# A Fourier filter and a routed expert layer on one core: the turn and the inverse of the first two batches in separate PSUM banks, a shorter last chain of the list, and noise products in another order

## The chip, the cores and the metric

The kernel runs on one core of a Trainium2 chip. The metric is the device time of one execution in microseconds. The three runs of the kernel before took 2244.74, 2246.81 and 2250.58 us, so the median is 2246.81 us. A profile of one more execution is used throughout; its times are counted from the start of its span.

## What is computed

The reference filters eight batches of 2496 x 256 numbers in the Fourier domain, and then sends each of the 19968 rows to two of eight experts:

```python
X = np.fft.rfft(x, axis=1)
y = np.fft.irfft(X * (filt_r + 1j * filt_i), n=x.shape[1], axis=1)
x = y.reshape(B * S, D)
logits = x @ w_gate
noise_scale = np.log1p(np.exp(x @ w_noise))
noisy_logits = logits + noise_scale * noise
top2 = the two largest of noisy_logits in each row
weights = softmax over these two
out[row] += weight * (relu(x[row] @ w1[e]) @ w2[e])   # for both experts e of the row
```

## The kernel before, in words

**Work and stages.** The transform of 2496 points is cut into 39 x 64. A batch passes a first DFT matmul (`s1`, names q1 and u3 in the profile), a second one with the filter (`kg1`, q3), the way back through the 64 points (`kg2`, q4, into the tile G), and then `t3` (q5: the *turn*, four transposes of G, evicted by ScalarE as `tf`) and `i2` (q6: the *inverse* DFT, evicted by ScalarE as `yt`, and written to `y` in DRAM). `t3` is line 512 on TensorE, `i2` is line 534. `gate` then takes the logits of a batch (`lg`, line 493), adds the scaled noise, finds the two experts of each row and their weights, counts rows (`rs`), and needs three tiny matmul groups on the way: `rk` (lines 812 to 814, ranks and counts), `sl` (883 and 884, first slots of blocks) and `st` (908, the table of slots). Behind them, VectorE copies the table to `tabi` (line 916), which SyncE and GpSimd read. `route` builds the batch's list of rows with comparisons (`oc`) and matmuls (`ra`), transposes it (line 957), finishes it on VectorE (lines 962 to 966) and scatters it to the DRAM tensor `lst` from GpSimd (line 969). `expert` reads lists, gathers rows, and runs both matmuls of an expert on blocks of 512 rows (lines 123 to 125 by way of `_mm3`, and 1210 and 1211).

**What sets the order.** The first two batches are transformed ahead of the first expert. Their work is written out in `fft_stream` in a table of slots: for slot `t` the functions in `plan[t]` are called in turn, and `pin` keeps every engine's instructions in the order in which they are written. Batch 0 has its turns and inverses in slots 12 to 17, batch 1 in slots 26 to 31. The gate of batch 1 is called in slot 26, with `hold=False`: its instructions are not held to that order, and a scheduler, which simulates the program, places them among the others. In that same slot `gating_more` is called until `rk`, `sl` and `st` have been written out too. So their PSUM tiles are allocated in slot 26, ahead of those of slot 27.

**PSUM.** There are eight banks, in four pools: `hps` with 2, `yps` with 2, `xps` with 1 and `fps` with 3. For the first two batches `EARLY` and `MOVES` say in which pool a name has its bank; a name that stands in neither has `fps`. `lg`, `u2`, `rk`, `sl`, `st` and `ra` are such names. `MOVES[14]` holds from slot 14 on, `MOVES[26]` from slot 26 on:

```python
EARLY = {"q1": "hps", "q2": "hps", "q5": "yps", "q6": "yps", "u1": "xps", "u3": "hps"}
BANKS = {"hps": 2, "yps": 2, "xps": 1, "fps": 3}
self.banks.update(MOVES.get(t, {}))
```

A tile gets a bank of its pool when an earlier tile in that bank has been used for the last time; tiles of a pool are served in the order in which the program allocates them.

Of the kernel before, what the change touches and what calls it, by code (L numbers as in the profile page):

```python
# [10 lines left out]
F32 = mybir.dt.float32  # L11
# [5 lines left out]
ALU = mybir.AluOpType  # L17
# [36 lines left out]
LR = 128  # L54
NLR = 1536
VAIN = 1400
HR = 56
# [80 lines left out]
EARLY = {"q1": "hps", "q2": "hps", "q5": "yps", "q6": "yps", "u1": "xps", "u3": "hps"}  # L138
BANKS = {"hps": 2, "yps": 2, "xps": 1, "fps": 3}

MOVES = {0: {"q3": "yps"}, 12: {"q3": "fps"}, 14: {"q3": "yps", "q4": "yps", "q5": "hps", "q6": "hps"}, 26: {"q1": "xps", "q4": "fps", "q5": "yps", "q6": "yps"}}


class Moe:
# [412 lines left out]
    def fft_stream(self):  # L557
# [105 lines left out]
        for t in range(max(plan) + 1):  # L663
            self.banks.update(MOVES.get(t, {}))
            for g in plan.get(t, []):
# [78 lines left out]
    def gate(self, bt, lgp):  # L744

        nc, P, v = self.nc, self.P, self.nc.vector
        sh = [RP, NG, E]

        def t(nm, s=None, dt=F32):
            return P.tile(s or sh, dt, name=nm)  # L750

        lg = lgp[:RP, :352].rearrange("p (g e) -> p g e", e=16)
        noise = t("noise")
        nc.sync.dma_start(noise, self.io["noise"][bt])
        A, B = self.rank
        u, w, l, z = A[:, 17:], B[:, 16:], t("gl"), t("gz")
# [3 lines left out]
        nc.scalar.activation(l, w, AF.Ln)  # L760
        v.tensor_scalar_add(w, w, -1.0)
        v.tensor_single_scalar(z, w, 0.0, op=ALU.is_equal)
        v.tensor_add(l, l, z)
        v.tensor_add(w, w, z)
        v.reciprocal(w, w)
        v.tensor_mul(l, l, w)
        v.tensor_mul(l, l, u)
        v.tensor_mul(l, l, noise)
        nz = t("gz")
        v.tensor_add(nz, l, lg[:, :, 0:8])  # L770
        keyb = self.key[:RP].unsqueeze(1).to_broadcast(sh)
# [26 lines left out]
        src, o = A, B  # L798
        for k in 1, 2, 4, 8, 16:
            v.tensor_add(o[:, 16:38], src[:, 16:38], src[:, 16 - k:38 - k])  # L800
            src, o = o, src
        src, o = src[:, 16:38], A[:, 17:]
# [8 lines left out]
        q = self.ps("rk")  # L811
# [41 lines left out]
        ri, rf = t("ri", [HR, 1], I32), P.tile([HR, 1], F32, name="rf", bufs=2)  # L853
# [64 lines left out]
    def route(self, bt, hi, lo, row, rf):  # L918


        nc, P = self.nc, self.P

        def bc(a, n):
            return a.rearrange("p g i -> p (g i)").unsqueeze(1).to_broadcast([RP, n, 4])


        x, v = P.tile([128, LR], F32, name="rx"), nc.vector
        xs = x[:, :HR]
        lr, tv = self.half[:RP, :4 * LR].rearrange("p (l j) -> p l j", j=4), self.half[:RP, 4 * LR:]
        for g0 in range(0, NG, 4):  # L930
            q = self.ps("ra")[:, :HR]
            for g in range(g0, min(g0 + 4, NG), 2):
                t = P.tile([128, 1024], F16, name="oc", tag=("xh", "xl", "b")[g // 2 % 3], bufs=1)


                ol, vv = t[:RP, 0:4 * LR], t[:RP, 4 * LR:4 * LR + 4 * HR]
                if bt < 2:
                    ol, vv = (a.rearrange("p (l j) -> p l j", j=4) for a in (ol, vv))
                else:
                    ol, vv = (a.rearrange("p (j l) -> p l j", j=4) for a in (ol, vv))  # L940

                def w(a):
                    return a if bt < 2 else a.rearrange("p l j -> p j l")

                v.tensor_tensor(w(vv), w(lr[:, :HR]), w(bc(hi[:, g:g + 2], HR)), op=ALU.is_equal)
                v.tensor_mul(w(vv), w(vv), w(tv[:, 2 * g:2 * g + 4].unsqueeze(1).to_broadcast([RP, HR, 4])))
                v.tensor_tensor(w(ol), w(lr), w(bc(lo[:, g:g + 2], LR)), op=ALU.is_equal)
                for j in range(4):
                    n = RP if g + j // 2 < NG - 1 else QA
                    nc.tensor.matmul(q, ol[:n, :, j], vv[:n, :, j], start=(g == g0 and j == 0), stop=(j == 3 and g + 2 >= min(g0 + 4, NG)))  # L950
            if g0 == 0:
                v.tensor_copy(xs, q)
            else:
                v.tensor_add(xs, xs, q)
            yield
        q = self.ps("ra")[:HR, :LR]
        nc.tensor.transpose(q, xs, self.ident)
        x = x[:HR]


        o = P.tile([HR, LR], F32, name="ro", **(dict(tag="th", bufs=3) if bt < 2 else dict(tag="ut1", bufs=1)))
        v.tensor_single_scalar(o, q, 0.0, op=ALU.not_equal)
        v.scalar_tensor_tensor(o, lr[:HR, :, 0], rf, o, op0=ALU.add, op1=ALU.mult)
        v.tensor_sub(o, q, o)
        v.tensor_single_scalar(x, q, 0.0, op=ALU.is_gt)
        v.tensor_sub(o, o, x)
        self.made = bt
        yield
        s = nc.gpsimd.indirect_dma_start(
            out=self.lst, out_offset=bass.IndirectOffsetOnAxis(ap=row[:, 0:1], axis=0),  # L970
            in_=o, in_offset=None, compute_op=ALU.add)
        for r in self.reads:
            self.tc.declare_no_dep(s.ins, r.ins, reason="what is read was complete a batch ago")
        self.writes.append((bt, s))
        yield
# [66 lines left out]
    def take(self, ent):  # L1042

        xg, at, ra = ent[2]
        gate = self.P.tile([128, 4, 1], F32, name="gt", bufs=3)[:, :len(xg)]
        self.nc.gpsimd.tensor_copy(gate, self.picked(ent)[:, :, D:][:, :, bass.ds(ra, 1)])
        return gate
# [287 lines left out]
```

## Time and profile before

| | us |
|---|---|
| median of 3 runs | 2246.81 |
| profiled execution, its device time | 2249.04 |
| its span, first to last instruction | 2247.3 |
| TensorE busy | 2202.3 |
| VectorE busy | 1614.5 |
| ScalarE busy | 1227.9 |
| GpSimd busy | 945.7 |

Busy time is that in which an engine has an instruction running. PE stands for TensorE, DVE for VectorE, ACT for ScalarE, POOL for GpSimd and SP for SyncE. A row of a timeline gives the start in us, the time from the start of the first to the end of the last instruction of the row, the engine, the line of the kernel, the operation, the tile written and the tiles read, their sizes, and how many instructions the row holds; in brackets stands how long the engine had been idle before it, and what ended that. The granted clock is the share of TensorE's full clock that it was given.

### The profile page before, as it was taken

How to read it: one execution, taken by the hardware profiler on the slowest of the kernel's cores; microseconds unless marked ns; L12 is line 12 of the kernel's file. 1: busy time of each engine (PE TensorE's matmuls, PEld its weight loads, DVE VectorE, ACT ScalarE, POOL GpSimd, SP SyncE). 2: the span in 40 equal slices, each digit the busy share in tenths (PEclk: the TensorE clock that was granted, in tenths of full speed). 3: DMA queues.
4: the chain of work that ended last, by engine and by line, in shares of the span. 5: the costliest groups of instructions: out<-in, count | busy, mean ns of one | idle time of the engine just before them, and what ended most of it. 6: DMA issues, size and time to landing. Idle time of an engine off the chain costs nothing.

```text
span 2247.3 us, 39485 instructions
## 1 busy us (share of the span) xinstructions
PE 2202.3 (98%) x12687; PEld 1847.3 (82%) x12687; DVE 1614.5 (72%) x3482; ACT 1227.9 (55%) x2415; POOL 945.7 (42%) x824
## 2 busy tenths in 40 slices
PE   8999999999999999999999999999999999999998
PEld 6658888888888888888888888878888888888887
DVE  4777778779877968797668857796555556667776
ACT  6475655665565456545554445544444344557776
POOL 4014335334433543444434534444545454544442
PEclk9999999999999999999999999999999999999999
DMA  8768778987887677666665657556555557787774
GB/s 246 229 198 221 190 174 182 211 212 166 196 195 180 150 167 170 142 158 155 145 153 125 147 116 174 111 124 122 110 125 114 126 109 156 154 209 201 208 197 127
DMA packets 435434, 370.57 MB, mean 165 GB/s; under 512 B 185643, under 2 KB 345363, under 8 KB 435219
## 3 DMA queue, kind: packets, MB, share of 16 engines
q1 hardware_dynamic: 373907, 283.58, 46.7%
q0 software_dynamic: 61312, 84.40, 23.4%
q8 instruction: 101, 1.65, 0.3%
q14 instruction: 114, 0.93, 0.1%
HBM read 227.73 MB, written 105.25 MB: 148 GB/s over the span
## 4 chain that ended last, share of the span: by engine, by line
PE 89%; DVE 3%; DMA 3%; ACT 2%; issue 2%; SPq 0%; POOL 0%; another core or an unknown queue 0%; POOLq 0%; DVEq 0%; ACTq 0%
PE yps L1210 20%; PE hps L123 13%; PE hps L125 13%; PE hps L124 12%; PE yps L1211 10%; PE q L446 3%; PE yps L125 3%; PE yps L123 3%; PE yps L124 3%; PE q L512 1%; DMA stage<-w 1%; PE u L459 1%; PE q L536 1%; PE q L329 1%; PE q L534 1%
## 5 line engine op out<-in xcount | busy, mean ns | idle before, releaser
L1218 POOL DMA_INDIRECT out<-stage,ids x316 | 535.7, 1695 | 415.8 <-DVE stage L1217 224.4
L1210 PE MATMUL yps<-w,hh 128*128 128x512 f32 x1952 | 690.2, 398 | 4.0 <-DVE stage L1217 2.6
L1027 POOL DMA_INDIRECT stage<-y,ids x316 | 328.5, 1040 | 582.8 <-DMA xt<-stage 424.6
L124 PE MATMUL hps<-mxl,w1h 128*128 128x512 f32 (+2 forms) x1424 | 529.7, 374 | 1.5 <-DVE mxl L1091 1.5
L123 PE MATMUL hps<-mxh,w1h 128*128 128x512 f32 (+2 forms) x1424 | 518.9, 377 | 5.2 <-DVE hl L1182 3.7
L125 PE MATMUL hps<-mxh,w1l 128*128 128x512 f32 (+2 forms) x1424 | 523.9, 370 | 0.0
L1211 PE MATMUL yps<-w,hl 128*128 128x256 f32 x1952 | 521.7, 281 | 0.0
L1182 DVE SCALAR_TENSOR_TENSOR hl<-hps,hh 128x512 fp32r<-128x512 f32 (+2 forms) x712 | 433.5, 624 | 97.4 <-ACT hh L1181 88.1
L1181 ACT ACTIVATE hh<-hps 128x512 fp32r<-128x512 f32 (+2 forms) x712 | 381.5, 555 | 183.4 <-PE hps L125 163.6
L1210 PEld LDWEIGHTS yps<-w,hh 128*128 128x128 f32 x1952 | 356.7, 188 | 82.2 <-issue 5.3
L1211 PEld LDWEIGHTS yps<-w,hl 128*128 128x128 f32 x1952 | 367.1, 188 | 26.3 <-issue 0.6
L1215 ACT ACTIVATE stage<-yps,gt 128x256 f32<-128x256 f32 x316 | 142.3, 478 | 348.9 <-PE yps L1211 177.8
L125 PEld LDWEIGHTS hps<-mxh,w1l 128*128 128x128 f32 x1424 | 268.0, 188 | 48.1
L123 PEld LDWEIGHTS hps<-mxh,w1h 128*128 128x128 f32 x1424 | 263.4, 188 | 50.5 <-DVE hl L1182 9.1
L124 PEld LDWEIGHTS hps<-mxl,w1h 128*128 128x128 f32 x1424 | 268.1, 188 | 42.8 <-DVE mxl L1091 2.0
L1217 DVE SCALAR_TENSOR_TENSOR stage<-yps,gt,stage 128x256 f32<-128x256 f32 x244 | 112.1, 479 | 215.7 <-ACT stage L1215 185.3
L1137 ACT CAST w1h<-stage 128x512 fp32r<-128x512 f32 x192 | 119.2, 622 | 113.2 <-DMA stage<-w 52.9
L1138 DVE TENSOR_TENSOR w1l<-stage,w1h 128x512 fp32r<-128x512 f32 x192 | 130.8, 686 | 56.7 <-ACT w1h L1137 46.6
L123 PE MATMUL yps<-w,hh 128*128 128x256 f32 x576 | 163.4, 288 | 4.0 <-ACT hh L1181 3.0
L125 PE MATMUL yps<-w,hl 128*128 128x256 f32 x576 | 159.2, 285 | 1.1 <-DVE hl L1182 1.1
L124 PE MATMUL yps<-w,hh 128*128 128x256 f32 x576 | 160.1, 284 | 0.0
L1138 DVE TENSOR_TENSOR w<-stage,w 128x512 fp32r<-128x512 f32 x228 | 152.7, 685 | 6.7 <-ACT w L1137 5.3
(231 smaller groups left out, 3044.4 us busy)
## 6 DMA issues: line engine op xcount, KB each, us to landing
stage<-w SPq DMA_DIRECT2D x420, 256.0 KB
x<-x SPq DMA_DIRECT2D x88, 256.0 KB
wb<-w SPq DMA_DIRECT2D x18, 1024.0 KB
fx<-fd SPq DMA_DIRECT2D x140, 128.0 KB
fd<-c SPq DMA_DIRECT2D x73, 240.0 KB
out<-z SPq DMA_DIRECT2D x24, 702.0 KB
y<-yt SPq DMA_DIRECT2D x40, 248.6 KB
y<-yt SPq DMA_DIRECT2D x40, 234.0 KB
```

Of the source, the lines that this page charges most:

```text
L123: nc.tensor.matmul(o, lh, rh, start=start, stop=False)
L124: nc.tensor.matmul(o, lh, rl, start=False, stop=False)
L125: return nc.tensor.matmul(o, ll, rh, start=False, stop=stop)
L1027: self.pin(lambda: nc.gpsimd.indirect_dma_start(out=x.bitcast(I32), out_offset=None, in_=self.y[:BLK + ready * ROWS], in_offset=bass.Indir ...
L1137: nc.scalar.copy(h, sv)
L1138: nc.vector.tensor_sub(l, sv, f32v(h))
L1181: r = nc.scalar.activation(h, p, AF.Relu)
L1182: v = nc.vector.scalar_tensor_tensor(l, p, 0.0, f32v(h), op0=ALU.max, op1=ALU.subtract)
L1210: nc.tensor.matmul(bank, h, hl, start=(f == 0), stop=False)
L1211: self.mm = nc.tensor.matmul(p, l, hl[:, 0], start=False, stop=(f == 7))
L1215: nc.scalar.activation(o, p, AF.Copy, scale=gate[:, t])
L1218: a = nc.gpsimd.indirect_dma_start(out=self.io["out"][:BLK + ready * ROWS], out_offset=bass.IndirectOffsetOnAxis(ap=ids[:, t:t + 1], axis= ...
```

## The change

It has three parts. From slot 14 the turn (q5) has its bank in `xps` in place of `hps`, and from slot 26 in `fps` in place of `yps`; the inverse (q6) stays in `hps` and then `yps`. In `gate` the factor 1/(w - 1) is multiplied with `u` and with the noise before it meets the logarithm. In `route` the sum of position and row offset is formed ahead of the transpose, and behind the transpose three instructions stand in place of five.

```diff
-MOVES = {0: {"q3": "yps"}, 12: {"q3": "fps"}, 14: {"q3": "yps", "q4": "yps", "q5": "hps", "q6": "hps"}, 26: {"q1": "xps", "q4": "fps", "q5": "yps", "q6": "yps"}}
+MOVES = {0: {"q3": "yps"}, 12: {"q3": "fps"}, 14: {"q3": "yps", "q4": "yps", "q5": "xps", "q6": "hps"}, 26: {"q1": "xps", "q4": "fps", "q5": "fps", "q6": "yps"}}
...
         nc.scalar.activation(l, w, AF.Ln)
         v.tensor_scalar_add(w, w, -1.0)
         v.tensor_single_scalar(z, w, 0.0, op=ALU.is_equal)
-        v.tensor_add(l, l, z)
         v.tensor_add(w, w, z)
         v.reciprocal(w, w)
+        v.tensor_mul(w, w, u)
+        v.tensor_mul(w, w, noise)
+        v.tensor_add(l, l, z)
         v.tensor_mul(l, l, w)
-        v.tensor_mul(l, l, u)
-        v.tensor_mul(l, l, noise)
...
+        o = P.tile([HR, LR], F32, name="ro", **(dict(tag="th", bufs=3) if bt < 2 else dict(tag="ut1", bufs=1)))
+        v.tensor_scalar(o, lr[:HR, :, 0], rf, None, op0=ALU.add)
         q = self.ps("ra")[:HR, :LR]
         nc.tensor.transpose(q, xs, self.ident)
         x = x[:HR]
-        o = P.tile([HR, LR], F32, name="ro", **(dict(tag="th", bufs=3) if bt < 2 else dict(tag="ut1", bufs=1)))
-        v.tensor_single_scalar(o, q, 0.0, op=ALU.not_equal)
-        v.scalar_tensor_tensor(o, lr[:HR, :, 0], rf, o, op0=ALU.add, op1=ALU.mult)
+        v.scalar_tensor_tensor(x, q, 0.0, o, op0=ALU.not_equal, op1=ALU.mult)
+        v.scalar_tensor_tensor(o, q, 0.0, x, op0=ALU.is_gt, op1=ALU.add)
         v.tensor_sub(o, q, o)
-        v.tensor_single_scalar(x, q, 0.0, op=ALU.is_gt)
-        v.tensor_sub(o, o, x)
```

Beside what the diff shows, the change moves instructions on the engines. The first place is TensorE in slots 26 and 27, in the second batch's turns and inverses. Before, the turns and inverses go on behind the two matmuls of line 329 (q1 and u3, the first DFT of the third batch):

```order
L534 MATMUL q6_1320<-tf_1306,cm_84 117x512
L329 MATMUL q1_1326<-x_1101,cm_84 120x512
L329 MATMUL u3_1331<-x_1103,cm_84 120x512
L512 MATMUL q5_1420<-ident_70,G_974 120x128 x4
L534 MATMUL q6_1427<-tf_1318,cm_84 117x512
L512 MATMUL q5_1432<-ident_70,G_974 120x128 x4
L534 MATMUL q6_1439<-tf_1425,cm_84 117x512
```

The matmuls of `rk` of the same batch stand behind ten more rows, among the first expert's transposes (xps); `sl` and `st` stand later still, among that expert's matmuls:

```order
L1087 MATMUL xps_1759<-ident_70,stage_83 128x128 x4
L512 MATMUL q5_1484<-ident_70,G_1128 120x128 x4
L812 MATMUL rk_1336<-rs_1280,small_77 117x8
L813 MATMUL rk_1336<-rs_1280,small_77 128x8
L814 MATMUL rk_1336<-small_77,rs_1280 8x1
L534 MATMUL q6_1491<-tf_1467,cm_84 117x512
```

In the changed kernel, at the same place on TensorE as in the first of these two:

```order
L534 MATMUL q6_1319<-tf_1305,cm_84 117x512
L329 MATMUL q1_1325<-x_1100,cm_84 120x512
L329 MATMUL u3_1330<-x_1102,cm_84 120x512
L812 MATMUL rk_1335<-rs_1279,small_77 117x8
L813 MATMUL rk_1335<-rs_1279,small_77 128x8
L814 MATMUL rk_1335<-small_77,rs_1279 8x1
L883 MATMUL sl_1393<-new_1386,small_77 8x1
L884 MATMUL sl_1393<-new_1386,small_77 8x1
L908 MATMUL st_1414<-sval_1403,small_77 1x64
L512 MATMUL q5_1419<-ident_70,G_973 120x128 x4
L534 MATMUL q6_1426<-tf_1317,cm_84 117x512
L512 MATMUL q5_1431<-ident_70,G_973 120x128 x4
```

All three groups of the gate have moved ahead of the fourth turn of the batch.

The second place is VectorE in the gate of the second batch, from w - 1 to the sum with the logits (`rank38` and `rank39` hold w and u, `gl` the logarithm, `w1l` the low halves of the first expert's weights). Before:

```order
L761 TENSOR_SCALAR rank38_95<-rank38_95 117x176
L762 TENSOR_SCALAR gz_1242<-rank38_95 117x176
L763 TENSOR_TENSOR gl_1241<-gl_1241,gz_1242 117x176
L764 TENSOR_TENSOR rank38_95<-rank38_95,gz_1242 117x176
L765 RECIPROCAL rank38_95<-rank38_95 117x176
L1138 TENSOR_TENSOR w1l_1738<-stage_83,w1h_1737 128x512
L1138 TENSOR_TENSOR w1l_1742<-stage_83,w1h_1741 128x512
L766 TENSOR_TENSOR gl_1241<-gl_1241,rank38_95 117x176
L767 TENSOR_TENSOR gl_1241<-gl_1241,rank39_94 117x176
L768 TENSOR_TENSOR gl_1241<-gl_1241,noise_1239 117x176
L1138 TENSOR_TENSOR w1l_1746<-stage_83,w1h_1745 128x512
L770 TENSOR_TENSOR gz_1254<-gl_1241,lg_1235 117x176
```

And in the changed kernel:

```order
L761 TENSOR_SCALAR rank38_95<-rank38_95 117x176
L762 TENSOR_SCALAR gz_1241<-rank38_95 117x176
L763 TENSOR_TENSOR rank38_95<-rank38_95,gz_1241 117x176
L767 TENSOR_TENSOR gl_1240<-gl_1240,gz_1241 117x176
L764 RECIPROCAL rank38_95<-rank38_95 117x176
L765 TENSOR_TENSOR rank38_95<-rank38_95,rank39_94 117x176
L766 TENSOR_TENSOR rank38_95<-rank38_95,noise_1238 117x176
L1137 TENSOR_TENSOR w1l_1736<-stage_83,w1h_1735 128x512
L768 TENSOR_TENSOR gl_1240<-gl_1240,rank38_95 117x176
L1137 TENSOR_TENSOR w1l_1740<-stage_83,w1h_1739 128x512
L770 TENSOR_TENSOR gz_1253<-gl_1240,lg_1234 117x176
```

The sum of the logarithm with its correction stands one place later, the products with u and the noise stand on w, and of four weight differences two have left this stretch.

The third place is VectorE at the end of the same gate in the changed kernel, where the table of slots (`tab`, `tabi`) is made from `st`; `G_1913` is the tile that the fifth half batch will write:

```order
L946 TENSOR_TENSOR oc_1595<-oc_1595,half_78 117x224
L897 TENSOR_SCALAR off_3686<-done_88 8x1
L913 TENSOR_TENSOR tab_93<-tab_93,st_1414 1x64
L902 TENSOR_SCALAR sval_3685<-small_77 8x32
L916 CAST tabi_1417<-tab_93 1x64
L1137 TENSOR_TENSOR w1l_1744<-stage_83,w1h_1743 128x512
L1137 TENSOR_TENSOR w1l_1748<-stage_83,w1h_1747 128x512
L438 MEMSET G_1913 128x80
```

The other two weight differences and the memset of G, which before stood within the gate's chain, stand behind the table here; the first three groups of the list's comparisons (`oc`) stand ahead of it.

## The prediction

> **What bounds the kernel now.** I read the page first (span, busy shares), then a table of busy time by stretch, then TensorE's own waits, and last the timelines of the engines around the one place where the change moves much.
>
> ```profile
> span 2247.3 us, 39485 instructions
> PE 2202.3 (98%) x12687; PEld 1847.3 (82%) x12687; DVE 1614.5 (72%) x3482; ACT 1227.9 (55%) x2415; POOL 945.7 (42%) x824
> ```
>
> TensorE (PE) is busy for 2202.3 of 2247.3 us, so 45 us of idle time are all that reordering can win, and any idle time that is added lengthens the run, unless a later wait shrinks for it. The stretches (columns: length, then busy us of PE, PEld, DVE, ACT, POOL, then PE's granted clock):
>
> ```profile
> 77.30:79.30 2.00, 1.98 (x12) 1.07 (x11) 1.81 (x10) 1.97 (x5) 0.00 (x0) 0.83 0.45 127
> 79.30:82.70 3.40, 3.15 (x9) 1.54 (x8) 2.96 (x24) 1.98 (x4) 0.00 (x0) 0.60 0.83 244
> 121.70:140.10 18.40, 14.17 (x55) 7.19 (x54) 13.41 (x42) 16.24 (x26) 6.86 (x10) 0.91 0.78 223
> 140.10:160.00 19.90, 19.90 (x93) 13.09 (x91) 15.47 (x76) 16.56 (x31) 0.85 (x2) 1.00 0.67 207
> 200.00:240.00 40.00, 36.80 (x240) 31.11 (x239) 28.08 (x44) 24.72 (x47) 20.57 (x22) 1.00 0.92 223
> 280.00:320.00 40.00, 37.78 (x256) 33.15 (x255) 27.40 (x59) 22.62 (x46) 15.69 (x13) 1.00 0.72 161
> 320.00:400.00 80.00, 76.68 (x518) 67.81 (x517) 70.72 (x185) 42.34 (x83) 38.75 (x29) 1.00 0.87 187
> 600.00:1000.00 400.00, 399.70 (x2290) 336.15 (x2289) 319.13 (x682) 224.03 (x431) 165.97 (x137) 1.00 0.73 168
> ```
>
> From 600 to 1000 us PE idles for 0.30 us in 400. There is nothing to win there, and a delay that arrives there stays to the end. What can still move lies in the first 400 us: 4.23 us idle at 121.7 to 140.1, and 3.20 + 2.22 + 3.32 = 8.7 us in the three later rows. The wait that the bank split speaks to is this row of PE's waits in the first 330 us:
>
> ```profile
> PE q L534 <- ACT yt L546: 3.2, 6, 0.9
> ```
>
> So the inverse (L534) waits 3.2 us in all for ScalarE to empty the bank it is to write.
>
> **The bank split, slots 14 to 25.** The turn (q5) leaves the two hps banks for xps, and the inverse (q6) has hps to itself there: it no longer needs the bank whose copy is still running. At most a part of the 3.2 us goes. But right behind these slots PE waits for VectorE's gate chain of the first batch:
>
> ```profile
> 77.08 0.37 PE L812 MATMUL rk<-rs,small 117*117 117x8 f32 x2 [1.69 <-DVE rs L796]
> ```
>
> If PE arrives sooner here, it waits longer. I take 0 to 0.7 us of gain up to this row.
>
> **The bank split from slot 26.** Here q5 goes to fps. That is where the gate's own small outputs live: the logits (lg), the ranks (rk) and two slot sums (sl, st). All of them are allocated in slot 26, when the gate of the second batch is written out, so before the q5 of slot 27. fps has three banks. rk, sl and st take all three, and the next q5 can have a bank only when rk has been used. The scheduler has therefore put rk, sl and st on PE ahead of that q5 (the orders in the section on the change). PE issues in order: all of its work behind these three now waits for the end of the gate chain. Before, that work ran while the chain was under way:
>
> ```profile
> 119.95 1.02 PE L329 MATMUL q<-x,cm 117*120 117x512 f32 x2
> 120.81 1.02 PE L329 MATMUL u<-x,cm 117*120 117x512 f32 x2
> 121.66 0.60 PE L512 MATMUL q<-ident,G 128*120 128x128 f32 x4
> 125.59 0.65 PE L512 MATMUL q<-ident,G 128*120 128x128 f32 x4 [2.21 <-ACT tf L517]
> 136.27 0.28 PE L812 MATMUL rk<-rs,small 117*117 117x8 f32 x2
> 146.97 0.19 PE L883 MATMUL sl<-new,small 8*8 8x1 f32 x2
> 157.01 0.27 PE L908 MATMUL st<-sval,small 8*1 8x64 f32 x2
> ```
>
> In the changed order PE comes to rk right behind the two L329, at about 121.7, and may go on to the next L512 only after st. So I need the earliest time of st. It is a chain on VectorE, which also works in order. Its rows, for the second batch first, then for the first batch where that one ran with less between:
>
> ```profile
> 120.96 0.35 ACT L760 ACTIVATE gl<-rank 117x176 f32<-117x176 f32 x1
> 121.34 0.25 DVE L761 TENSOR_SCALAR rank<-rank 117x176 f32<-117x176 f32 x1 [1.41 <-issue]
> 123.80 1.22 DVE L1138 TENSOR_TENSOR w1l<-stage,w1h 128x512 fp32r<-128x512 f32 x2
> 127.05 0.69 DVE L1138 TENSOR_TENSOR w1l<-stage,w1h 128x512 fp32r<-128x512 f32 x1 [1.02 <-ACT w1h L1137]
> 131.28 0.12 DVE L438 MEMSET G<- 128x80 f32 x1 [1.69 <-PE q L512]
> 135.01 0.46 DVE L796 TENSOR_REDUCE rs<-rank 117x8 f32<-117x176 f32 x1
> 73.14 0.18 DVE L803 TENSOR_SCALAR gs<-ge 117x22 f32<-117x22 f32 x1 [0.46 <-ACT ge L790]
> 73.96 0.33 DVE L807 TENSOR_TENSOR dense<-oh,gs 117x176 f32<-117x176 f32 x1
> 81.51 0.13 DVE L878 CAST new<-ci 8x1 f32<-8x1 int32 x1
> 85.19 0.20 DVE L842 SCALAR_TENSOR_TENSOR lo<-hi,df 117x44 f16<-117x44 f16 x1
> 85.31 0.64 DVE L945 TENSOR_TENSOR oc<-half,hi 117x224 f16<-117x224 f16 x3
> 86.87 0.14 DVE L885 TENSOR_TENSOR st<-nblk,sl 8x1 f32<-8x1 f32 x1
> 86.94 0.62 DVE L946 TENSOR_TENSOR oc<-oc,half 117x224 f16<-117x224 f16 x3
> 88.17 0.69 DVE L424 TENSOR_TENSOR ab<-q,fr 128x512 f32<-128x512 f32 x1
> 90.17 0.22 DVE L904 TENSOR_SCALAR sval<-sge,small 8x32 f32<-8x32 f32 x1
> ```
>
> 1. Start: the logarithm ended at 121.31. In the new order u2 and lg stand ahead of most of the turns, and the small copies for lg ahead of the turns' copies on ACT, so it may end up to 1.3 us sooner. I take 120.6 (120.0 to 121.3).
> 2. To rs: 121.34 to 135.47 was 14.1 us. Out of it go the waits of 1.02 and 1.69 (the second pair of weight differences and the memset of G now stand behind st) and that pair, 1.2. Into it come the combine weights (L803 to L809, six instructions of 0.1 to 0.3, some 1.1, and the 0.46 wait ahead of them), which before stood behind rs. That is 11.8 us: rs at 132.4, rk at 132.5.
> 3. rk to new: in the first batch 77.08 to 81.64, 4.6 us. So sl at 137.1, and VectorE has it at 137.4.
> 4. sl to sval: 86.87 to 90.39 was 3.5 us, of which the pair at L424 and L425 (1.2) and the three L946 (0.6) were other work: 1.7. The new order puts list positions and three groups of list comparisons of the same batch between them (four small instructions, 0.8, and from 85.31 to 86.87 with the L946 behind, 2.1): 4.6 in all. So sval at 142.0, st done at 142.3.
>
> PE starts the L512 that it began at 121.66 at 142.3, then: 20.6 us later, less 1.0 for rk, sl and st, which it has behind it. From this comes off what it lost before in the same work: 4.23 us of idle time, and the slow clock, 18.4 x (1 - 0.91) = 1.7. On comes what the restart costs. After the wait of 1.69 at 77.08 the clock fell to 0.83 and 0.60, which cost 2.0 x 0.17 + 3.4 x 0.40 = 1.7 us; I take 1.7 again, and 1.0 for waits on ACT, whose copies from here to the first expert add up to about what PE has to do. So PE is 20.6 - 1.0 - 4.2 - 1.7 + 1.7 + 1.0 = 16.4 us late at the first expert's matmuls.
>
> The page "TensorE: Matmul & The Clock Gate" of the Trainium skill (Part 1, the HAM clock gate) says that the array falls to half rate only after about 3.4 us of idleness and needs about as long at work to come back. The long wait would cost 1.7 us by it too, but the earlier waits of 1.69 and 2.21 would not have slowed the clock, so the 1.7 of before would stay and the delay be 18.1. The rows of this trace show the slow clock right behind a wait of 1.69, so I go by the rows.
>
> Of the 8.7 us that PE idles between 200 and 400, some may vanish because VectorE and ACT are ahead: I give back 1.4 (0 to 4). **Sum: +15 us.**
>
> **What moves with it on other queues.** SP and POOL read the slot table behind st (L916), and these reads now stand earlier in their queues: on SP ahead of the writes of y and the w2 loads, on POOL ahead of the second block's gathers. Behind a table ready at 142.7 that holds up only work that needs PE's restart anyway; I cost it at 0, at most 2 where a w2 load becomes late.
>
> **The gate's products.** The step w - 1 (L761) overwrites what the logarithm reads, so it cannot start before it ends: the rows at 120.96 and 121.34 show it 0.03 us behind. The two products stand behind w - 1 in the chain. So nothing is formed beside the logarithm; nine VectorE instructions stood behind it and nine stand there now. I cost it at 0, plus or minus one of them, 0.4.
>
> **The list's last chain.** Five steps behind the transpose become three:
>
> ```profile
> 109.69 0.28 DVE L962 TENSOR_SCALAR ro<-ra 56x128 f32<-56x128 f32 x1 [0.61 <-PE ra L957]
> 110.90 0.28 DVE L966 TENSOR_TENSOR ro<-ro,rx 56x128 f32<-56x128 f32 x1
> 111.51 1.60 POOL L969 DMA_INDIRECT lst<-ro,row  x1 [62.87 <-DMA x<-x]
> ```
>
> 109.69 to 111.18 becomes about 1.0, so the first list comes some 0.5 us sooner. Its readers, the first expert's gathers and weights, are done long before PE restarts at 142.3: worth 0. Later lists come while PE has other experts queued (0.30 us idle in 400): 0.
>
> **The number.** On the profiled execution's 2249.04 us (span 2247.3 and 1.7 around it) +15 gives 2264; the median of the runs, 2246.81, lies 2.2 below that execution, so I say 2262. Bounds: start of the chain and its sum 1.8 sooner, 4 us regained in place of 1.4, no waits on ACT: +10, 2257. Chain 1.7 longer, a second slow stretch of the clock (1.7), a late w2 (2): +20, 2267.
>
> **Rivals.**
> - Absorbed. The stall is there, but the idle time after it goes nearly all: VectorE, ACT and the DMAs run ahead during 20 us, and the 8.7 us between 200 and 400 go with it. Then 16.4 - 8.7 = +8, and with a chain 3 us shorter +5: 2252. Against it: the waits there hang on lists and gathers that PE's own order releases. 0.10.
> - Better, not slower. The banks are what counts: the waits of the inverse go (3.2) and the list comes 0.5 sooner, 2243. The point from which it decides: PE must find st ready by about 127, 121.7 and the 5.9 us that it lost before, with the gate chain under 7 us in place of 21. For it speaks only that the scheduler chose this order. The page "PSUM — Partial Sum Buffer" of the Trainium skill (Summary: rules for kernel authors) says to aim a matmul at another bank than the one being read, which is what this edit does; the row of 3.2 us agrees that it would pay here, and no more. 0.04.
> - Worse. The restart finds weights or gathers late, since SP stood behind the table. One landing of weights, as the chain that ended last has it:
>
> ```profile
> 120.07 2.36 DMA stage<-w
> ```
>
> Two or three such waits make +20 to +22, 2269 at the most. 0.08.
>
> About 0.3% (6.7 us) is what a measurement of this kernel can tell from no change. The likeliest case has 0.78; the range 2252 to 2269 also takes in most of the second and fourth. Slower by over 0.3%: 0.88 (the main case, the worse one, and a small part of the absorbed). Within 0.3%: 0.10. Faster by over 0.3%: 0.02.
>
> **What would show it.** In the profile after: a wait of PE at rk (the second L812) of about 10 us for rs, then about 4.5 at sl and 4.5 at st, all between 121 and 143; the next L512 behind st; from 400 us on the same idle time as before, all about 15 us later. VectorE's w - 1 still right behind the logarithm. The forecast is wrong if PE's second rk waits less than 5 us, or if the idle time between 160 and 400 falls by more than 6.

## The result and the profile after

The changed kernel takes 2269.95 us (median of 5 runs, 2263.77 to 2278.45), the kernel before beside it 2248.94 us (2244.74 to 2253.05): a ratio of 1.009 with a 95% interval of 1.007 to 1.011, some 21 us slower. The forecast was 2262, with a range up to 2269. Of the 8 us between them, 2.1 lie in the base: the forecast started from 2246.81, and the kernel before has 2248.94 now. The profiled execution has a device time of 2268.84 us. From its page:

```profile
span 2267.0 us, 39479 instructions
PE 2203.4 (97%) x12687; PEld 1847.7 (82%) x12687; DVE 1610.2 (71%) x3474; ACT 1228.3 (54%) x2415; POOL 951.5 (42%) x824
```

The span is 19.7 us longer and TensorE's busy time about 1, so some 18.5 us of it are idle time of TensorE. Its waits in the first 345 us (what it waited for, us in total, times, longest):

```profile
PE rk L812 <- DVE rs L796: 11.4, 2, 8.4
PE sl L883 <- DVE new L878: 4.1, 1, 4.1
PE st L908 <- DVE sval L904: 3.7, 1, 3.7
PE q L534 <- ACT yt L546: 0.8, 2, 0.7
```

The wait for yt has fallen from 3.2 to 0.8, as the bank split is made to do. Three waits of 16.2 us stand against it, and they are the second batch's rk and its sl and st, where the prediction put them. TensorE's timeline there:

```profile
122.68 1.02 PE L329 MATMUL u<-x,cm 117*120 117x512 f32 x2
132.07 0.53 PE L812 MATMUL rk<-rs,small 117*117 117x8 f32 x2 [8.37 <-DVE rs L796]
137.27 0.18 PE L883 MATMUL sl<-new,small 8*8 8x1 f32 x2 [4.11 <-DVE new L878]
141.24 0.37 PE L908 MATMUL st<-sval,small 8*1 8x64 f32 x2 [3.74 <-DVE sval L904]
141.54 1.11 PE L512 MATMUL q<-ident,G 128*120 128x128 f32 x4
```

The L512 that started at 121.66 before starts at 141.54, 19.9 us later. What follows is seen best by stretches that begin at this same piece of work. Before (length, then busy us of PE, PEld, DVE, ACT, POOL, then PE's granted clock):

```profile
121.70:141.80 20.10, 15.87 (x61) 8.24 (x60) 14.62 (x47) 17.81 (x29) 7.52 (x10) 0.92 0.80 231
141.80:400.00 258.20, 248.27 (x1598) 213.74 (x1597) 204.91 (x480) 153.28 (x291) 99.89 (x86) 1.00 0.81 193
400.00:600.00 200.00, 198.56 (x1299) 174.54 (x1298) 163.70 (x343) 115.87 (x226) 82.51 (x71) 1.00 0.85 195
600.00:2000.00 1400.00, 1397.27 (x7513) 1168.59 (x7512) 980.82 (x2015) 698.74 (x1338) 623.70 (x526) 1.00 0.66 145
```

After, with the stall itself as the first row:

```profile
123.70:141.54 17.84, 1.62 (x13) 1.25 (x12) 16.88 (x90) 3.19 (x6) 0.46 (x3) 0.61 0.21 63
141.54:160.00 18.46, 18.18 (x67) 10.48 (x67) 3.92 (x9) 15.93 (x28) 3.81 (x4) 0.92 0.55 157
160.00:420.00 260.00, 248.54 (x1598) 212.97 (x1597) 197.99 (x424) 153.29 (x292) 97.84 (x88) 1.00 0.79 191
420.00:620.00 200.00, 197.25 (x1278) 173.14 (x1277) 162.18 (x343) 114.36 (x222) 85.10 (x69) 0.99 0.83 193
620.00:2020.00 1400.00, 1397.36 (x7517) 1168.86 (x7516) 977.95 (x2008) 698.61 (x1337) 630.38 (x526) 1.00 0.67 145
```

TensorE's idle time, length less busy time, was 4.23, 9.93, 1.44 and 2.73 us in the four stretches of before. In the four behind the restart it is 0.28, 11.46, 2.75 and 2.64. The first stretch gave its idle time up. The next two, where the prediction gave 1.4 us back, hold 2.8 us more. Their largest waits, from 160 to 620 us:

```profile
PE hps L123 <- DVE hl L1181: 5.6, 6, 1.9
PE ra L950 <- DVE oc L946: 3.4, 2, 2.0
PE yps L123 <- ACT hh L1180: 2.2, 2, 1.4
```

Behind `route`, a line of the changed kernel has a number lower by one than before: hl is L1181 here and L1182 there. From 141.8 to 600 us of before neither of the first two is among the seven largest, which run from

```profile
PE yps L123 <- ACT hh L1181: 3.0, 4, 2.2
...
PE xps L1087 <- ACT stage L1078: 0.8, 1, 0.8
```

TensorE's largest waits there are now for VectorE, where they were for ScalarE. That comparison rests on two executions: in the run with gate and list alone, which has the banks of before, the largest wait there is for hl too, 2.6 us.

### The profile page after: what moved, and what is told of

It is laid out like the page before. It is cut to its first block, busy times and chain, and to the rows that moved or that the text cites. A ratio compares the mean times of both kernels' runs of the same rounds, so it can differ in the third digit from the quotient of the medians.

```text
span 2267.0 us, 39479 instructions
## 1 busy us (share of the span) xinstructions
PE 2203.4 (97%) x12687; PEld 1847.7 (82%) x12687; DVE 1610.2 (71%) x3474; ACT 1228.3 (54%) x2415; POOL 951.5 (42%) x824
## 4 chain that ended last, share of the span: by engine, by line
PE 90%; DVE 3%; ACT 2%; DMA 2%; issue 2%; SPq 0%; POOL 0%; another core or an unknown queue 0%; ACTq 0%; DVEq 0%; POOLq 0%
PE yps L1209 20%; PE hps L123 13%; PE hps L124 13%; PE hps L125 13%; PE yps L1210 10%; PE q L446 3%; PE yps L125 3%; PE yps L123 3%; PE yps L124 3%; PE q L512 2%; PE u L459 1%; PE q L536 1%; PE q L537 1%; PE q L538 1%; DMA stage<-w 1%
## 5 line engine op out<-in xcount | busy, mean ns | idle before, releaser
L123 PE MATMUL hps<-mxh,w1h 128*128 128x512 f32 (+2 forms) x1424 | 519.9, 377 | 9.3 <-DVE hl L1181 7.9
L1181 DVE SCALAR_TENSOR_TENSOR hl<-hps,hh 128x512 fp32r<-128x512 f32 (+2 forms) x712 | 433.0, 624 | 106.4 <-ACT hh L1180 100.0
L123 PEld LDWEIGHTS hps<-mxh,w1h 128*128 128x128 f32 x1424 | 263.7, 188 | 56.1 <-DVE hl L1181 14.9
L1137 DVE TENSOR_TENSOR w1l<-stage,w1h 128x512 fp32r<-128x512 f32 x192 | 130.6, 685 | 58.6 <-ACT w1h L1136 50.8
L123 PE MATMUL yps<-w,hh 128*128 128x256 f32 x576 | 163.7, 288 | 3.8 <-ACT hh L1180 2.2
L1137 DVE TENSOR_TENSOR w<-stage,w 128x512 fp32r<-128x512 f32 x228 | 152.3, 684 | 5.9 <-ACT w L1136 5.2
```

Of the source, the lines that this page charges most:

```text
L123: nc.tensor.matmul(o, lh, rh, start=start, stop=False)
L1137: nc.vector.tensor_sub(l, sv, f32v(h))
L1181: v = nc.vector.scalar_tensor_tensor(l, p, 0.0, f32v(h), op0=ALU.max, op1=ALU.subtract)
```

## The experiments

**The theories.** A, the prediction's: from slot 26 q5 shares fps with rk, sl and st, this puts the three ahead of the fourth turn on TensorE, and TensorE then waits for VectorE's gate chain. The rivals: the loss lies in the edits of gate and list; it needs both bank moves; or the pool itself costs, wherever rk, sl and st stand. Each group of runs has its own runs of the kernel before beside it, on one chip, so ratios are given; "us slower" is the ratio's share of that chip's median of before.

**The two bank moves alone** (the kernel before with the changed line of MOVES):

```diff
-MOVES = {0: {"q3": "yps"}, 12: {"q3": "fps"}, 14: {"q3": "yps", "q4": "yps", "q5": "hps", "q6": "hps"}, 26: {"q1": "xps", "q4": "fps", "q5": "yps", "q6": "yps"}}
+MOVES = {0: {"q3": "yps"}, 12: {"q3": "fps"}, 14: {"q3": "yps", "q4": "yps", "q5": "xps", "q6": "hps"}, 26: {"q1": "xps", "q4": "fps", "q5": "fps", "q6": "yps"}}
```

The four runs that follow take one part of this line or the rest of the change.

> Both bank moves, with the gate and the list as before. Theory A (TensorE stands behind rk, sl and st of the second batch, since the turn of slot 26 shares fps with them; the gate's and the list's edits are worth nothing): the whole loss of the changed kernel, 17 to 23 us over before; TensorE waits of about 8 us at the second rk, 4 at sl, 4 at st. Rival B (part of the loss comes from the gate's and the list's new order on VectorE, felt in later batches): the waits are there, but the time is only 12 to 15 us over before. Rival C (the split of slot 14 costs by itself): no different from A here.

Measured: 2253.23 us beside 2235.21, ratio 1.0076 [1.0061, 1.0091], 17 us slower. Between 119 and 146 us TensorE waits 4.1 at sl, 3.7 at st, and at rk

```profile
PE rk L812 <- DVE rs L796: 9.4, 1, 9.4
```

The loss and the three waits are those of the changed kernel. The banks alone make them, but for a wait at rk that is 1.0 longer.

**The edits of gate and list alone** (the changed kernel with the line of MOVES of before).

> The gate's and the list's edits alone, banks as before. Theory A: no change, within 4 us of before; no TensorE wait at the second rk; the logarithm's end and VectorE's w - 1 still 0.1 us apart; the last chain of the first list 1.0 us in place of 1.5. Rival B: 4 to 7 us slower than before.

Measured: 2235.16 us, ratio 1.0004 [0.9994, 1.0014]. They are worth nothing that shows.

**The move of slot 14 alone** (the kernel before with q5 in xps from slot 14).

> Only the turn's move of slot 14 (hps to xps). Theory A: no change, within 4 us; the inverse's waits for yt between 62 and 83 us fall from 1.6 to under 0.3, and TensorE's wait at the first rk grows from 1.7 to about 3, so that nothing is won. Rival C: 2 to 4 us slower, with more idle time of TensorE between 60 and 122.

Measured: 2232.23 us, ratio 0.9985 [0.9976, 0.9993], 3.4 us faster. That this split costs something is ruled out; that it gains, theory A had not expected. Up to the first batch's rk nothing is won. TensorE comes 1.3 us sooner and waits 1.3 longer. Its wait at rk is to be held against the prediction's row at 77.08 with 1.69; the run with gate and list alone, on this chip, has its rk at 77.21 too, behind 1.69. With the move of slot 14:

```profile
77.21 0.37 PE L812 MATMUL rk<-rs,small 117*117 117x8 f32 x2 [2.99 <-DVE rs L796]
```

The gain comes behind it, where the first batch's list is matched. The scheduler has moved its L950 from between L459's sixteen matmuls to behind them. In the run with gate and list alone, as before:

```profile
99.95 0.79 PE L459 MATMUL u<-G,wg 128*32 128x360 f32 x2
100.68 0.38 PE L950 MATMUL ra<-oc 117*128 117x56 f16 x4
100.99 0.80 PE L459 MATMUL u<-G,wg 128*32 128x360 f32 x4
101.72 0.60 PE L950 MATMUL ra<-oc 117*128 117x56 f16 x8
102.26 1.00 PE L459 MATMUL u<-G,wg 128*32 128x360 f32 x10
103.19 0.70 PE L407 MATMUL q<-fx,cm 128*128 128x512 f32 x1
```

With the move of slot 14 alone:

```profile
99.19 1.41 PE L459 MATMUL u<-G,wg 128*32 128x360 f32 x16
100.53 0.61 PE L950 MATMUL ra<-oc 117*128 117x56 f16 x8
100.96 1.10 PE L407 MATMUL q<-fx,cm 128*128 128x512 f32 x2
```

In one piece the sixteen take 1.34 us; in three pieces they and twelve L950 take 3.24. The first L459 comes 0.76 us sooner with the move (99.19 and 99.95), the next L407 2.23 sooner (100.96 and 103.19). At the next L459 (114.03 and 111.84) 2.2 us remain. The other 1 us or so of the 3.4 was not traced.

**All but the move of slot 26** (the changed kernel with q5 left in yps from slot 26).

> The changed kernel with the turn of slot 26 left in yps, as before. Theory A: the loss is gone, within 4 us of before, no TensorE wait at the second rk, at sl or at st. Rival B or C: still 3 to 7 us slower than before.

Measured: 2232.16 us, ratio 0.9985 [0.9975, 0.9995]. The whole loss hangs on one word in MOVES[26]; without it the change is 3.4 us faster. This and the run before it are the fastest versions found.

**The move of slot 26 alone.**

> The kernel before with the move of slot 26 alone (q5 to fps); slot 14, gate and list as before. Theory A (the move of slot 26 puts rk, sl and st ahead of the second batch's fourth turn, and the split of slot 14 is a separate gain of some 3 us): 17 to 22 us slower than the kernel before, more than with both moves, with waits of some 9 us at the second rk, 4.1 at sl and 3.7 at st. Rival (the loss needs both moves, since the split from slot 14 brings TensorE to this place at another time): less than 12 us slower.

Measured: 2253.29 us beside 2234.78, ratio 1.0091 [1.0077, 1.0106], 20 us slower, with waits of 8.4, 4.1 and 3.7. So the loss does not need both moves. Within the noise the two moves add up: 20.3 less 3.4 is 16.9, and both together gave 17.0. That the sum fits to 0.1 us is luck: the interval of the 20.3 goes from 17.2 to 23.7, that of the 17.0 from 13.6 to 20.3, and they were taken on two chips.

**rk, sl and st one slot later, banks as changed.** In the slot loop:

```diff
-            if gating:
+            if gating and t >= (0, 26 + 1)[gating[0]]:
```

> The changed kernel with its banks untouched, but rk, sl and st of the second batch are allocated one slot later, so behind two more turns. On TensorE two turns, two inverses and two matmuls of L329 now stand ahead of rk, some 5 us of work. Theory A (the order counts): the wait at the second rk falls from 8.4 to about 3, those at sl and st stay at 4.1 and 3.7; 12 to 14 us slower than the kernel before, where both bank moves alone gave 18. Rival (the bank counts: turns that share fps with the gate's outputs wait for them wherever these stand): 16 to 20 us slower.

Measured: 2247.78 us, ratio 1.0059 [1.0045, 1.0072], 13 us slower, in theory A's range. TensorE still waits 4.1 at sl and 3.8 at st; at rk:

```profile
134.06 0.56 PE L812 MATMUL rk<-rs,small 117*117 117x8 f32 x2 [5.73 <-DVE rs L796]
```

The wait at rk has fallen by 2.6 only, to 5.7 and not to about 3, because VectorE's chain ends some 2 us later too: the other two weight differences (L1137, at 126.91 and 127.78) stand in it again. So A had the total right and this wait wrong.

**Two and five slots later** (26 + 2 and 26 + 5 in that line).

> As the run with one slot, but two slots later: four more turns stand ahead of rk, and rk, sl and st then stand among the first expert's matmuls, 4 to 9 us of work apart. Theory A: no wait over 1 us at any of the three; between 4 us faster and 2 us slower than the kernel before. Rival (the bank counts): 16 to 20 us slower still.

> As the run with one slot, but five slots later: all turns of the second batch stand ahead of rk. Theory A: no wait at rk, sl or st; between 4 us faster and 2 us slower than the kernel before, unless the second batch's table and lists, now made some 20 us later, are waited for, which would show as new waits of TensorE for gathers or lists between 200 and 400 us and cost a few us. Rival (the bank counts): 16 to 20 us slower still.

Measured: 2245.39 us, ratio 1.0051 [1.0038, 1.0065], and 2243.32 us, ratio 1.0044 [1.003, 1.0058], so 11 and 10 us slower. Both theories miss. None of the three waits is left in either run, so by A the loss should be gone; by the rival it should have stayed whole. With two slots, TensorE's waits in the first 345 us show what came instead:

```profile
PE xps L1086 <- ACT stage L1077: 3.9, 1, 3.9
PE xps L1086 <- ACT c L378: 3.2, 1, 3.2
```

With turns that run ahead, TensorE waits for ScalarE's copies, and the first expert's transposes wait for the one bank of xps, in which q1 still stands. The changed kernel does not show these; its stall lies ahead of them. How much of the 11 us belongs to q5 in fps and how much to the later gate, which also moves the third batch's work among the experts, these runs do not separate.

**The changed kernel again, and with a longer chain.** The second adds 20 instructions to the gate of the second batch:

```diff
-        v.tensor_add(nz, l, lg[:, :, 0:8])
+        v.tensor_add(nz, l, lg[:, :, 0:8]); [v.tensor_scalar_mul(nz, nz, 1.0) for _ in range(20 * (bt == 1))]
```

> The changed kernel itself, beside the other runs of this call. Both bank moves alone were 17 to 18 us slower than the kernel before and the edits of the gate and the list alone made no difference, so 16 to 20 us slower, if the edits add up; the profile of before and after on the first chip had the spans 19.7 apart.

> The changed kernel with 20 more VectorE instructions in the gate chain of the second batch (each multiplies the noisy logits by 1.0, 0.29 us apart by the row of w - 1, so 5.8 us in all), which lengthens the wait at rk and nothing else. Nothing is regained after the restart: 5.3 to 6.3 us slower than the changed kernel. Part is regained, as the prediction's 1.4 of 16.4 and up to 4: 3 to 5.3 us slower. Absorbed by idle time between 200 and 400 us: 0 to 3 us slower.

Measured: 2263.94 us beside 2245.78, ratio 1.0086 [1.0072, 1.01], 19 us slower; and with the longer chain 2271.38, ratio 1.0123 [1.0107, 1.0138], 7.4 us more than without. The medians put it above the range of "nothing is regained". The traces of the two show the added stall itself. The 20 instructions on VectorE, and TensorE's rk and restart behind them:

```profile
125.80 5.70 DVE L770 TENSOR_SCALAR gz<-gz 117x176 f32<-117x176 f32 x20
```

```profile
137.68 0.53 PE L812 MATMUL rk<-rs,small 117*117 117x8 f32 x2 [14.71 <-DVE rs L796]
...
147.16 1.11 PE L512 MATMUL q<-ident,G 128*120 128x128 f32 x4
```

Without them the restart is at 141.36, 5.80 us sooner. An output scatter of an expert some 1090 us later, without and with them:

```profile
1228.30 1.62 POOL L1217 DMA_INDIRECT out<-stage,ids  x1 [1.02 <-DVE m L780]
```

```profile
1234.08 1.62 POOL L1217 DMA_INDIRECT out<-stage,ids  x1 [1.03 <-DVE m L780]
```

It is 5.78 us later, so here nothing of the added stall is regained. On the way it was less: TensorE's first matmul of the third batch's logits (L493) comes 4.66 us later than without the chain (326.23 and 321.57), the fourth's 3.81 (528.60 and 524.79), the fifth's 5.78 again (734.51 and 728.73). The spans of the two profiles, 2266.8 and 2262.1, are 4.7 apart, and the medians 7.4. Absorption, 0 to 3 us, is ruled out; between nothing regained and a microsecond or so regained these runs do not decide.

**rk, sl and st in one bank** (early batches, banks as changed):

```diff
-        q = self.ps("rk")
+        q = self.gq = self.ps("rk")
...
-        q = self.ps("sl")
+        q = self.gq[:, 64:] if self.early else self.ps("sl")
...
-        q = self.ps("st")
+        q = self.gq[:, 128:] if self.early else self.ps("st")
```

> The changed kernel with rk, sl and st of a batch in one fps tile (columns 0, 64 and 128) in place of three: the next turns get a bank as soon as the one before is read, and sl and st stand three and five turns later on TensorE; rk still stands ahead of the fourth turn. Theory A, each wait worth its length: the wait at rk stays at 8 to 9, those of 4.1 and 3.7 at sl and st go, 7 to 8 us faster than the changed kernel. If only half of a removed wait comes off, as in the run with the gate two slots later, because waits for ScalarE's copies come in its place: 3 to 5 us faster. If the order of sl and st is worth nothing: 0 to 1 us.

Measured: 2256.45 us beside 2245.78, ratio 1.0055 [1.0041, 1.0068]; 7.5 us faster than the changed kernel measured beside it. Of the three waits the one at rk is left, and the turn goes on right behind it; sl and st follow at 138.75 and 143.48 without a wait:

```profile
131.65 0.53 PE L812 MATMUL rk<-rs,small 117*117 117x8 f32 x2 [9.25 <-DVE rs L796]
132.67 1.11 PE L512 MATMUL q<-ident,G 128*120 128x128 f32 x4
```

The waits of 4.1 and 3.7 are worth 7.5. As long as the wait at rk remains, a microsecond of the stall counts about once, as with the longer chain.

**Turn and inverse split without the gate's pool** (the end of the changed line of MOVES; slot 14 as changed):

```diff
-MOVES = {... 26: {"q1": "xps", "q4": "fps", "q5": "fps", "q6": "yps"}}
+MOVES = {... 26: {"q1": "xps", "q4": "fps", "q5": "xps", "q6": "yps"}}
```

> The changed kernel, but from slot 26 the turn goes to the bank xps in place of fps: turn and inverse are split all the same, and the gate's outputs keep fps to themselves (with the logits and q4). On TensorE rk stands behind the sixth turn, sl and st among the first expert's matmuls. Theory A (the loss comes from the pool shared with the gate's outputs, not from the split): a wait at rk under 4 us, none over 1 at sl and st; between 4 us faster and 5 us slower than the kernel before. Rival (any split of turn and inverse costs here, since the turns run ahead of ScalarE's copies): 10 us slower or more, with waits for tf, yt or c.

Measured: 2249.4 us, ratio 1.0019 [1.001, 1.0028], 4 us slower: within A's range, at its upper end. With all else the same, q5 in fps is 19 us slower than the kernel before, in xps 4 us slower, and in yps, where it was, 3.4 us faster. So some 15 of the 23 us between fps and yps belong to the gate's pool, and the other 8 are paid with q5 in xps as well: for that part the rival, that any split costs here, holds. The rows of what is left in this run are a wait for the bank of xps that q1 holds, and a shorter wait at rk:

```profile
123.54 0.66 PE L512 MATMUL q<-ident,G 128*120 128x128 f32 x4 [2.11 <-ACT c L378]
135.21 0.56 PE L812 MATMUL rk<-rs,small 117*117 117x8 f32 x2 [3.15 <-DVE rs L796]
```

## Why the prediction was right about the cause and too low about the size

**Where rk, sl and st stand.** Right. The changed kernel shows it, and so do the runs with one move each.

**The gate chain.** Right within 0.9 us at each step. rs was forecast for 132.4 and ended at 131.92, but two errors offset each other there: the logarithm ended 0.5 us later than the 120.6 taken, and the way from w - 1 to rs took 10.8 us, not 11.8. VectorE's rows:

```profile
121.10 0.25 DVE L761 TENSOR_SCALAR rank<-rank 117x176 f32<-117x176 f32 x1 [2.53 <-ACT gl L760]
131.46 0.46 DVE L796 TENSOR_REDUCE rs<-rank 117x8 f32<-117x176 f32 x1
```

rk was forecast for 132.5 and came at 132.07, sl for 137.1 and came at 137.27, the restart for 142.3 and came at 141.54.

**From the restart to the first expert.** Nearly right in its terms. The 4.2 us of idle time of before went (4.23 to 0.28), and the 1.0 of waits on ACT that was to come did not show. The clock is a draw as forecast: 0.92 over 20.1 us before, 0.92 over 18.46 after. By the rule of the page "TensorE: Matmul & The Clock Gate" of the Trainium skill (Part 1, the HAM clock gate), by which only some 3.4 us of idleness slow the array, the slow clock of before would have stayed, and the delay been 1.7 longer; the rows do not show that, with 1.6 us lost to the clock before (0.08 of 20.1) and 1.5 after (0.08 of 18.46). The place named was wrong: the first expert's first L123 comes at 156.02 in place of 151.79, only 4.2 us later, since in the new order it stands ahead of work that it stood behind. The third batch's first L493 is a better mark: 302.73 before, 318.55 after, 15.8 us later.

**The time given back.** This is the step that failed: "Of the 8.7 us that PE idles between 200 and 400, some may vanish because VectorE and ACT are ahead: I give back 1.4 (0 to 4)." Nothing came back; the idle time rose by 2.8 us, 1.5 from 160 to 420 and 1.3 from 420 to 620. So this term of the sum is off by 4.2 us. And a slow stretch of the clock follows right behind the waits of 1.95 for oc and 0.34 for hl at 593 and 595 us, where the kernel before has 1.00 throughout:

```profile
590.00:600.00 10.00, 7.71 (x40) 5.87 (x40) 8.95 (x20) 7.19 (x15) 7.41 (x5) 0.83 0.68 106
```

That is another 1.7 us (10 x 0.17). The prediction had named such a second stretch, for its upper bound only. The first L493 shows both: 15.8 us late in the third batch, 17.65 in the fourth (505.11 and 522.76), 19.43 in the fifth (711.63 and 731.06). A second pair of profiles agrees: the changed kernel measured again, against the run with gate and list alone, is 17.2, 20.2 and 19.3 late at the same three places.

The reason given does not hold for ScalarE: while TensorE stalls, ACT is busy 3.19 of 17.84 us. It has nothing to copy, since TensorE produces nothing. VectorE did get ahead: it is busy with the chain, and then has less to do than before while the turns are caught up, 7.55 us in place of 22.56. The first 28 us from the same L512, in the kernel before and in the changed one:

```profile
121.70:150.00 28.30, 24.07 (x95) 13.67 (x94) 22.56 (x95) 23.84 (x40) 7.71 (x11) 0.94 0.85 253
```

```profile
141.54:170.00 28.46, 26.74 (x100) 15.82 (x100) 7.55 (x15) 21.94 (x38) 3.99 (x5) 0.95 0.59 175
```

But the later waits are for what VectorE makes out of TensorE's own output or behind it in order. hl is formed from hps, and the comparisons (oc) that TensorE waits for at 593 us start late because VectorE itself had stood idle for TensorE:

```profile
591.05 0.39 DVE L945 TENSOR_TENSOR oc<-half,hi 117x224 f16<-117x224 f16 x1 [3.85 <-PE yps L125]
```

So the lead was of no use to these waits. Why they are 2.8 us longer than before, and not the same, the runs do not show. The longer chain agrees: of 5.80 us of stall added, 5.78 are there 1090 us later, and 4.7 at the end of the spans.

**The sum.** Measured by the same terms: 19.9 for the restart, less 1.0 for rk, sl and st, less 3.95 up to 160 us, plus 2.8 behind it, less 0.1 from 620 to 2020 us and 0.3 from there to the end (14.77 us idle before, 14.50 after), is 17.4. The spans are 19.7 apart. The other 2.3 us are busy time: from the restart to 2020 us TensorE is busy 1861.3 us, before it was 1860.0 with the 1.0 of rk, sl and st in it. Of this, 1.7 is the slow stretch at 590 to 600 us; the cause of the 0.6 left was not found. The forecast had +15 by these terms. The miss of 4.7 is 4.2 for the time given back and 2.3 of busy time, less some 2 for the smaller terms: the restart 0.7 sooner, and the waits on ACT that did not come.

**Slot 14.** Right up to the first batch's rk (0 of the 0 to 0.7). The 2.2 us behind it were not foreseen. In the changed kernel they lie ahead of the stall, where they can at most start the chain sooner: with both moves st comes at 140.06, with the move of slot 26 alone at 141.74. The loss is 3.3 us smaller with both, but the two intervals overlap.

**Gate, list, tables.** Right: nothing. w - 1 (L761 above) still waits for the logarithm. The list's last chain takes 0.91 us (107.81 to 108.72) in place of the prediction's 1.49 (109.69 to 111.18), and the run with gate and list alone is as fast as the kernel before.

**The rivals.** "Absorbed" and "better" fell. "Worse" came out in size, not in mechanism: the loss is as large, but the largest waits behind the restart are for VectorE (hl, oc) and ScalarE (hh), not for weights or gathers. The rule of the page "PSUM — Partial Sum Buffer" of the Trainium skill (Summary: rules for kernel authors), another bank than the one being read, is borne out in the waits from slot 14 (those for yt between 60 and 84 us fall from 1.1 to 0.2 in the run with that move alone) and not in the time from slot 26 (with slot 14 moved: 4 us slower in xps, 19 in fps, 3.4 faster without a split): there the other bank had an owner that held it longer than the copy did. The 3.4 us of slot 14 do not come from those waits, which the waits for tf and at rk make up for (tf 0.2 to 0.9, rk 1.7 to 3.0), but arise behind them, in part from the other order of L950.

## What to carry to other kernels

Before moving a tile to another pool, list who else allocates there, and how long each holds its bank. A tiny matmul at the end of a long chain on another engine must not be a tile that the next big matmul needs to be rid of: an engine that issues in order turns it into a stall of the chain's length. And count such a stall in full, or nearly so. ScalarE, which the stalled engine feeds here, had little to do meanwhile; idle time seen later is not a reserve unless a row shows that its releaser would have been early.

## What was not expected of the hardware

- Small matmuls of other operands set between matmuls of one kind cost more than their own time: the sixteen of L459 with twelve L950 between them took 3.24 us, where the sixteen in one piece took 1.34, and eight L950 behind them 0.43. Twelve are 0.65 by that, so some 1.2 us lie at the four changes from one to the other. What takes them there no row shows.
- The granted clock can fall behind waits as short as 1.7 us (the prediction's rows at 77 us), and behind shorter ones that add up. In the changed kernel, ahead of the stall, no wait is over 0.91 us, but TensorE is busy for only 2.00 of 3.40 us, and the next stretch is slow:

```profile
113.90:117.30 3.40, 2.00 (x15) 1.36 (x13) 2.45 (x12) 0.77 (x3) 0.00 (x0) 1.00 0.75 243
117.30:120.70 3.40, 3.40 (x11) 2.15 (x11) 0.25 (x1) 2.71 (x4) 1.63 (x3) 0.51 0.57 162
```

It does not fall each time. The wait of 1.91 for hl at 241.35, with full work around it, leaves it at 1.00:

```profile
240.00:260.00 20.00, 18.65 (x116) 15.11 (x117) 14.32 (x23) 13.44 (x27) 7.20 (x10) 1.00 0.77 211
```

Behind the wait of 3.2 us at xps in the run with the gate two slots later:

```profile
137.40:143.60 6.20, 6.04 (x16) 4.57 (x17) 4.76 (x28) 1.69 (x4) 1.74 (x2) 0.50 0.91 254
```

The clock is 0.50 for 6.2 us of matmuls, so this wait of 3.2 costs another 3.1. A longer wait need not cost more: in the changed kernel, behind 17.84 us with 1.62 of work, it is 0.92 on the mean of 18.46 us, a loss of 1.5.
